# Pinning the loads in need order, folding the second DFT axis once more, a one-step inverse root, and a new stage order in a Sinkhorn attention, Fourier mixing and MLP kernel

## The chip, the cores and the metric

The kernel runs on one core of one Trainium2 chip. The metric is the device time of one execution in microseconds (us), lower is better. Each version was executed several times, and medians are quoted. A profile is of one execution, whose span can differ by some us from the median of the timed ones (before: span 369.3, median 371.6).

The engines are called as in the profile: PE is TensorE (matmuls), PEld its weight loads, DVE is VectorE, ACT is ScalarE, POOL is GpSimd and SP is SyncE. GpSimd and SyncE are the two engines that issue transfers here, each through its own queue.

## The reference, cut to what matters

Four batches, eight heads, a sequence of 768 in 8 blocks of 96, head width 64. A Sinkhorn iteration on `sort_net` gives block weights P, with which the blocks of k and v are mixed. Attention runs within each block. Its output, laid out as 768 x 512 per batch, goes through a two-dimensional Fourier transform (the real part is kept), a residual, a normalisation and an MLP.

```python
for _ in range(5):                       # Sinkhorn, (4, 8, 8, 8)
    P = exp(P - max(P)); P = P / sum(P, -1); P = P / sum(P, -2)
k_sorted = einsum('bhij,bhjcd->bhicd', P, k_b)
v_sorted = einsum('bhij,bhjcd->bhicd', P, v_b)
attn = softmax(q_b @ k_sb.T / 8)         # 96 x 96 in each block
x = (attn @ v_sb) -> (4, 768, 512)
mixed = real(fft(fft(x, axis=1), axis=2))
u = x + mixed
un = (u - mean(u)) / sqrt(var(u) + 1e-6)
out = u + relu(un @ w_ch1) @ w_ch2       # 512 -> 2048 -> 512
```

## The kernel before: the parts that matter

The program is written as a set of generators (attention, FFT with normalisation, MLP, value mix), and at build time a scheduler that simulates the engines decides the order of the instructions on each engine. Each engine then runs its list strictly in that order. An instruction may be held to the place where it was written with `tc.keep_in_program_order`. The kernel before never uses this, so the scheduler places its loads too.

The loads of the kernel before, in the order written. The 514 KB table `tab`, which the Fourier transform of the block means needs, and the first weights come late in the program text.

```python
pw  <- sort_net                                   # SyncE
def load_qk(b, hf):                               # GpSimd: half of one batch's k, then q, 384 KB each
    ...nc.gpsimd.dma_start(t..., src[b, 4*hf:4*hf+4]...)
load_qk(0, 0)
idh, idf, cm, cmh                                 # SyncE, small constants
for n in range(8):                                # SyncE, v of batches 0 and 1 (first half of the rows)
    nc.sync.dma_start(v32[hf][:, 12*qq:12*qq+12, :], vv[0:128, 12*n:12*n+12, :])
cdb, sdb, erow, vrow                              # SyncE, tables of the second DFT and others
load_qk(0, 1)
csa, sna, lt, rrow                                # SyncE; L240 loads lt, L243 one row of rb (rrow)
# ... Sinkhorn, block mean, value mix ...
tab = cload("tab", [128, 2, 2, 257], F32)         # SyncE, the last table written
# ... in the attention of batch 0:
if (b, hp) == (0, 2):
    for c in range(4): nc.gpsimd.dma_start(w1sb[:, c, :], ...)        # 512 KB each
    for c in range(4): nc.gpsimd.dma_start(w2sb[:, 4*c:4*c+4, :], ...)
# [...]
v1[hf] <- second half of v's rows                 # SyncE, for batches 2 and 3
```

The code calls the second half of v's rows "v1", the prediction "batch 1's v". It is the second pair of batches.

The second DFT, one product of 128 rows at a time (24 in the whole kernel), accumulates five 512-wide matmuls in one PSUM bank. PSUM is TensorE's output memory:

```python
ps = pf([128, DM])                                              # DM = 512
nc.tensor.matmul(ps, lt[:, 128*T:128*T+128], rb, start=True, stop=False)
for c in range(4):
    lh = ys[c][g][:, 128*tt:128*tt+128]
    rh = cdb[:, c, :] if c < 2 else sdb[:, c - 2, :]
    nc.tensor.matmul(ps, lh, rh, start=False, stop=(c == 3))     # L725
u = rt[:, T, :] * RSC + ps                                       # VectorE, L728
bn_stats, bn_aggr                                                # VectorE
```

The inverse root of the normalisation is a Newton chain on 128x3 values, three small steps on VectorE and then on GpSimd:

```python
nc.gpsimd.tensor_scalar(x, x, -0.5, None, op0=ALU.mult)
for _ in range(3):
    nc.gpsimd.tensor_tensor(z, y, y, op=ALU.mult)
    nc.gpsimd.tensor_tensor(z, z, x, op=ALU.mult)
    nc.gpsimd.tensor_scalar(z, z, 1.5, None, op0=ALU.add)
    nc.gpsimd.tensor_tensor(y, z, y, op=ALU.mult)
nc.gpsimd.tensor_tensor(z, mv[:, :, 0], y, op=ALU.mult)
nc.gpsimd.tensor_scalar(nm, z, -1.0, None, op0=ALU.mult)         # L680
```

The second half of v is prepared on VectorE (a tree of additions for the block mean, then eight subtractions of it, L873), and no MLP work is emitted before that is done.

The softmax here doesn't subtract the row's maximum and nothing guards it: scores larger than these inputs give would overflow.

## Time and profile before

| | before |
|---|---|
| median of the timed runs | 371.64 us (370.59 to 373.28, 4 runs) |
| TensorE busy | 305.4 us, 83% of the span |
| VectorE busy | 220.8 us |
| first MLP matmul starts at | 129.58 us |
| from there to the end | 240 us, TensorE busy 230 |

The head of the page has one line of busy times, with the share of the span and the number of instructions, and then rows in which each digit is the busy share of one fortieth of the span (9.2 us) in tenths. In the row PEclk the digits are the granted TensorE clock in tenths of full speed. The page of the kernel before:

```profile
PE 305.4 (83%) x2452; PEld 186.0 (50%) x2452; DVE 220.8 (60%) x507; ACT 138.5 (38%) x249; POOL 43.7 (12%) x155
...
PE   0989500864885789999998999998999999999995
...
PEclk9998955775589699999999999999999999999999
```

The row PE has a hole in slices 6 and 7, counted from 1, and is full from slice 16 on. The clock falls to 5 in and after the hole. The view of stretches (windows) of the same kernel gives busy times by engine; the number in brackets counts instructions, and the last three columns are the granted clock, the DMA share and the bandwidth:

```profile
core 0: us, PE busy (x) PEld busy (x) DVE busy (x) ACT busy (x) POOL busy (x), PEclk, DMA share, GB/s
0.00:42.00 42.00, 29.75 (x248) 20.26 (x248) 25.25 (x72) 22.50 (x40) 11.66 (x26) 0.96 1.07 238
42.00:65.00 23.00, 0.11 (x1) 0.14 (x2) 0.65 (x1) 0.67 (x1) 0.00 (x0) 0.57 0.87 226
65.00:130.00 65.00, 45.97 (x515) 33.27 (x516) 51.20 (x112) 34.79 (x62) 7.75 (x21) 0.73 0.29 44
130.00:369.30 239.30, 229.55 (x1691) 132.36 (x1689) 143.68 (x324) 80.55 (x147) 24.25 (x108) 1.00 0.11 33
```

From 42 to 65 us the engines do next to nothing while the transfers run at 226 GB/s. From 130 us on TensorE is busy for 96% of the time: there only less TensorE work helps. What TensorE waited for, longest first (engine, tile and line, what released it: total us, times, longest):

```profile
PE pf_575 L508 <- DMA tab_sb<-k_tab: 23.1, 1, 23.1
PE pm_139 L252 <- DMA v_82<-in_v_dram: 9.8, 1, 9.8
PE pf_1268 L704 <- ACT un_1250 L692: 5.5, 1, 5.5
```

The 23 us hole is one wait for one table. The chain of waits, the work that ended last followed backwards, gives start, duration and what; "SPq" is the queue of SyncE:

```profile
27.77 7.63 SPq L243
...
36.55 14.09 SPq L243
50.68 14.07 DMA tab_sb<-k_tab
...
96.08 5.21 DVE vcx L873 x6
...
121.44 0.82 ACT un_1250 L692
```

The table was issued at 50.68 us only, and needed 14.07 us to land. Ahead of it in SyncE's list stand the issues of two rows of 1 KB each (L243), and issuing them took 7.63 and 14.09 us: the engine stood in the issue itself. The list of transfers (what, issuing queue, KB each, median us from issue to landing) shows what else was under way:

```profile
w1sb<-in_moe_w_ch_dram POOLq DMA_DIRECT2D x4, 512.0 KB, 23.4
w2sb<-in_moe_w_ch_dram POOLq DMA_DIRECT2D x4, 512.0 KB, 32.3
...
k_70<-in_k_dram POOLq DMA_DIRECT2D x1, 384.0 KB, 5.6
```

The scheduler hoisted the MLP weights, written in the middle of attention 0, to 5.3 to 22.5 us of GpSimd's list, 100 us before they are used and ahead of batch 1's k and q. So 4 MB of weights share the transfer engines with everything needed in the first 50 us. Last, the timeline of GpSimd around the first inverse root (start, duration, engine, line, operation, tile):

```profile
117.33 0.19 POOL L675 TENSOR_TENSOR nz_1113<-ny_1112 128x3 f32<-128x3 f32 x1
...
121.17 0.23 POOL L680 TENSOR_SCALAR nm_1114<-nz_1113 128x3 f32<-128x3 f32 x1
```

The chain takes about 4.1 us from 117.33 us, and ScalarE's `un` at 121.44 waits for it. The timeline of TensorE in the second DFT of the last batch shows the pace of the 512-wide products. The duration of a pipelined matmul overlaps the next one, so the distance between starts is what it costs:

```profile
298.68 0.38 PE L725 MATMUL pf_3780<-vcx,yr_3539 128*128 128x512 f16 x1
298.90 0.38 PE L725 MATMUL pf_3780<-vcx,yr_3554 128*128 128x512 f16 x1
```

That is about 0.216 us each, and 1.08 us for five.

### The profile page before, as it was taken

Reading aid. Unit: us, or ns where it says so; the run is one execution under the profiler, and the core shown is the slowest. Engines: PE = TensorE matmul, PEld = TensorE weight load, DVE = VectorE, ACT = ScalarE, POOL = GpSimd, SP = SyncE. Lnnn points to the kernel's source line nnn. Section 1 sums busy time; section 2 is a strip of 40 time slices with the busy share of each in tenths; the row PEclk is TensorE's granted clock in tenths of the full one; section 3 lists DMA queues with packets and bytes.
Section 4 is the critical chain, followed back from the end, with each engine's and each line's share of the span. In section 5 each row is a group of like instructions: output and inputs, shape, how many; then the busy total and the mean of one; then the engine's idle time right before and its main releaser. Section 6 shows DMA issues by size and latency. Waiting matters only on the chain.

```text
span 369.3 us, 6087 instructions
## 1 busy us (share of the span) xinstructions
PE 305.4 (83%) x2452; PEld 186.0 (50%) x2452; DVE 220.8 (60%) x507; ACT 138.5 (38%) x249; POOL 43.7 (12%) x155
## 2 busy tenths in 40 slices
PE   0989500864885789999998999998999999999995
PEld 0448400752543667666643555664455555454552
DVE  3477500399988596447986644579473286563542
ACT  1647600371648688715302585630124212022100
POOL 7111000010004104000012300002011020021000
PEclk9998955775589699999999999999999999999999
DMA  8999987060335100514001101000100100100102
GB/s 155 320 265 225 210 219 250 27 105 0 44 45 66 22 0 6 83 57 78 9 0 58 41 2 51 36 2 0 59 28 3 58 28 2 57 30 28 57 2 85
DMA packets 18477, 25.95 MB, mean 70 GB/s; under 512 B 1737, under 2 KB 12685, under 8 KB 18449
## 3 DMA queue, kind: packets, MB, share of 16 engines
q0 software_dynamic: 11136, 10.49, 18.3%
q1 hardware_dynamic: 7314, 15.08, 11.5%
q8 instruction: 19, 0.31, 0.4%
q14 instruction: 8, 0.07, 0.1%
HBM read 29.37 MB, written 6.29 MB: 97 GB/s over the span
## 4 chain that ended last, share of the span: by engine, by line
PE 57%; DVE 19%; DMA 12%; SPq 7%; issue 2%; ACT 2%; POOL 1%; DVEq 0%; ACTq 0%
SPq L243 6%; DMA vcx<-k_sdb 4%; DMA tab_sb<-k_tab 4%; DMA v_82<-in_v_dram 2%; DVE vcx L873 2%; PE pm_3075 L773 1%; DVE r_540 L425 1%; PE pm_3013 L773 1%; PE pf_575 L508 1%; PE pm_2172 L773 1%; PE pm_2918 L773 1%; PE pm_4212 L773 1%; PE pm_2322 L773 1%; PE pm_3791 L773 1%; PE pm_4039 L773 1%
## 5 line engine op out<-in xcount | busy, mean ns | idle before, releaser
L756 PEld LDWEIGHTS <-w1sb 128*128 128x128 f16 x512 | 49.2, 98 | 36.6 <-issue 5.1
L508 PE MATMUL pf_575<-tab_sb,atp_537 128*64 128x129 f32 (+1 forms) x16 | 3.7, 405 | 23.1 <-DMA tab_sb<-k_tab 23.1
L465 PEld LDWEIGHTS <-vcx 128*128 128x128 f16 x128 | 18.1, 181 | 5.4 <-issue 2.3
L165 DVE CAST vsf<-pm_502 96x512 f16<-96x512 f32 x1 | 0.8, 799 | 27.7 <-PE pm_502 L468 27.7
L252 PE MATMUL pm_139<-v_82,idf_sb 128*128 128x512 f32 x12 | 7.7, 812 | 9.8 <-DMA v_82<-in_v_dram 9.8
L508 PEld LDWEIGHTS pf_575<-tab_sb,atp_537 128*64 128x64 f32 x16 | 3.1, 218 | 23.4 <-issue 23.4
L163 ACT CAST vsf<-pm_492 96x512 f16<-96x512 f32 x1 | 0.8, 786 | 25.2 <-PE pm_492 L468 25.2
L252 PEld LDWEIGHTS pm_139<-v_82,idf_sb 128*128 128x128 f32 x12 | 3.1, 267 | 13.6 <-issue 12.5
L468 PEld LDWEIGHTS <-vbn 128*128 128x128 f16 x64 | 8.7, 136 | 0.7 <-DVE bdv_1_291 L440 0.7
L773 PEld LDWEIGHTS <-hr_4077 128*128 128x128 f16 x48 | 4.7, 98 | 5.5
L773 PEld LDWEIGHTS <-hr_2224 128*128 128x128 f16 x48 | 4.7, 98 | 5.6
L773 PEld LDWEIGHTS <-hr_3663 128*128 128x128 f16 x48 | 4.7, 98 | 5.5
L773 PEld LDWEIGHTS <-hr_1704 128*128 128x128 f16 x48 | 4.6, 98 | 5.2
L773 PEld LDWEIGHTS <-hr_3127 128*128 128x128 f16 x48 | 4.6, 98 | 5.1
L773 PEld LDWEIGHTS <-hr_3898 128*128 128x128 f16 x48 | 4.6, 98 | 5.1
L692 ACT ACTIVATE un_3291<-u_2960,nm_3108,ny_3106 128x512 f16<-128x512 f32 x1 | 0.8, 813 | 16.8 <-POOL nm_3108 L680 16.8
L368 PEld LDWEIGHTS <-ksb_109 64*128 64x128 f16 x128 | 3.8, 97 | 6.5 <-issue 4.3
L413 PEld LDWEIGHTS <-ebuf_101 97*128 97x128 f16 x96 | 5.7, 108 | 2.6 <-DVE ebuf_101 L390 2.0
L692 ACT ACTIVATE un_2388<-u_2057,nm_2205,ny_2203 128x512 f16<-128x512 f32 x1 | 0.8, 813 | 16.5 <-POOL nm_2205 L680 16.5
L260 ACT CAST vcx<-v_82 128x768 f16<-128x768 f32 x4 | 3.3, 832 | 9.7 <-DMA v_82<-in_v_dram 9.7
L773 PEld LDWEIGHTS <-hr_3365 128*128 128x128 f16 x48 | 4.6, 98 | 4.5
L773 PEld LDWEIGHTS <-hr_2467 128*128 128x128 f16 x48 | 4.2, 98 | 4.7 <-issue 0.2
(1428 smaller groups left out, 896.4 us busy)
## 6 DMA issues: line engine op xcount, KB each, us to landing
w1sb<-in_moe_w_ch_dram POOLq DMA_DIRECT2D x4, 512.0 KB, 23.4
w2sb<-in_moe_w_ch_dram POOLq DMA_DIRECT2D x4, 512.0 KB, 32.3
v_82<-in_v_dram SPq DMA_DIRECT2D x4, 384.0 KB, 6.6
v_83<-in_v_dram SPq DMA_DIRECT2D x4, 384.0 KB, 13.2
v_524<-in_v_dram SPq DMA_DIRECT2D x2, 768.0 KB, 18.0
v_527<-in_v_dram SPq DMA_DIRECT2D x2, 768.0 KB, 18.9
tab_sb<-k_tab SPq DMA_DIRECT2D x1, 514.0 KB
k_70<-in_k_dram POOLq DMA_DIRECT2D x1, 384.0 KB, 5.6
```

What stands on the lines that cost most here:

```text
L243: nc.sync.dma_start(rb[96:97, :], cn["rrow"].ap())
L252: nc.tensor.matmul(psm.rearrange("p c d -> p (c d)"), idf, v32[n // 6][:, 8 * (n % 6):8 * (n % 6) + 8, :].rearrange("p c d -> p (c d)"), s ...
L260: nc.scalar.copy(vcp[:, 2 * n:2 * n + 2], v32[hf][:, 12 * qq:12 * qq + 12, :].rearrange("p (c r) d -> p c r d", r=6))
L368: nc.tensor.matmul(pss[h2][:, j, :], ks[rows, 4 * g + j].rearrange("p r c -> p (r c)"), qt[rows, :, cc])
L413: nc.tensor.matmul(po[:, 65 * T:65 * T + 96], e[:, S * g + 256 * tt + 128 * n: S * g + 256 * tt + 128 * n + 128], vsf[:, vi:vi + 96], star ...
L425: nc.vector.tensor_tensor(rt[:, :, D * h:D * h + D], po3[:, :, 0:D], rz[:, :, None].broadcast_to([128, 6, D]), op=ALU.mult)
L465: nc.tensor.matmul(ps[:, dd, :], vcx[:, :, d], bd, start=True, stop=(t == 1))
L468: nc.tensor.matmul(ps[:, dd, :], vbn[:, d:d + 1].broadcast_to([128, 128]), bd, start=False, stop=True)
L508: nc.tensor.matmul(psr[64 * o:64 * o + 64, cs], atp[:, par, c].rearrange("p b g -> p (b g)"), tab[:, o, c, cs], start=(c == 0), stop=(c == 1))
L756: nc.tensor.matmul(ps, w1sb[:, c, 128 * fc:128 * fc + 128], ut[:, c, :], start=(c == 0), stop=(c == 3))
L773: nc.tensor.matmul(ps, hr[:, fc, 128 * tt:128 * tt + 128], w2sb[:, fc, :], start=(fc == 0), stop=(fc == 15))
L873: nc.vector.tensor_tensor(vcp[:, 2 * n:2 * n + 2], v1[hf][:, 12 * qq:12 * qq + 12, :].rearrange("p (c r) d -> p c r d", r=6), vbs[1][:, 0: ...
```

## The change

Its stated intent has four parts: loads pinned in the order of need; the second DFT axis folded once more, with even and odd outputs computed apart; the inverse root by one GpSimd `pow`; and FFT 0 emitted ahead of attention 1. With the first part comes another treatment of the second half of v: it is loaded on GpSimd's queue behind the weights, in two halves of 1.5 MB through one buffer, cast on ScalarE, and its mean is taken out by extra matmuls instead of VectorE subtractions. The core of the diff, cut:

```diff
+    def start(ins):
+        return tc.keep_in_program_order(ins)
     load_qk(0, 0)
-    idh = cload(...) ; idf ; cm ; cmh
+    load_qk(0, 1)
+    pack ...                                  # the small constants in one transfer
-    for n in range(8):                        # v, 384 KB each
+    for n in range(4):                        # v, 768 KB each
         ...
+    start(nc.sync.dma_start(tab, cn["tab"].ap()))       # table, now ahead of the DFT's tables
+    start(nc.sync.dma_start(dtab, cn["dtab"].ap()))
     [...]
-                if (b, hp) == (0, 2): ...w1sb, w2sb...
     [...] after the Sinkhorn and the first half of the value mix:
     load_qk(1, 0)
     for n in range(16): v_mix(0, n)
+    for c in range(4): start(nc.gpsimd.dma_start(w1sb[:, c, :], ...))
+    load_qk(1, 1)
+    for c in range(4): start(nc.gpsimd.dma_start(w2sb[:, 4*c:4*c+4, :], ...))
     [...] second half of v:
+        for hf in range(2):
+            sv = wt([128, 48, D], F32, "hrB", 1, "v32")
+            start(nc.gpsimd.dma_start(sv, vv[128:256, 48*hf:48*hf+48]))
+            ... four casts on ScalarE, a tree of adds on VectorE (L865) ...
     [...] second DFT:
-            nc.tensor.matmul(ps, lt..., rb, start=True, stop=False)
             for c in range(4):
                 lh = ys[c][g][:, 128*tt:128*tt+128]
-                nc.tensor.matmul(ps, lh, rh, start=False, stop=(c == 3))
+                nc.tensor.matmul(ps[:, c % 2::2], lh, dtab[:, c, :],     # 256 wide, every second column
+                                 start=(c == 0), stop=False, ...)
+            nc.tensor.matmul(ps, lt..., rb, start=False, stop=True, ...)
     [...] inverse root:
-            (the Newton chain)
+            nc.gpsimd.tensor_scalar(mv[:, :, 1], mv[:, :, 1], 1e-6, None, op0=ALU.add)
+            nc.gpsimd.tensor_tensor(y, mv[:, :, 1], mhalf, op=ALU.pow)
+            nc.gpsimd.tensor_tensor(nm, mv[:, :, 0], y, op=ALU.mult)
+            nc.gpsimd.tensor_scalar(nm, nm, -1.0, None, op0=ALU.mult)
     [...] stage order:
+            while b == 1 and not gate1():     # m = 3: (0, 1) in uns, the second half of FFT 0 is normalised
+                yield None
```

The fold also adds VectorE steps in front of the first DFT (sums and differences of the lower and upper quarter of the axis), and moves scratch tiles into shared buffers to make room. One more thing differs: before, all MLP work is held at build time until the second half of v is ready; after, only the second group of batch 0 is.

## The prediction

> **What bounds it now.** Two regimes. From 130 us on TensorE is the limit: the table of stretches has it busy 229 of 239 us; the MLP alone costs 512 x 0.163 (four 384-wide matmuls take 0.65 us) + 384 x 0.216 = 166 us. Before 130 us it is busy only about 76 us, part of it at half clock. The list of waits gives 23.1 us in one wait for the 514 KB cosine/sine table (42 to 65 us; the clock falls to 0.50, as the Trainium skill, "TensorE: Matmul & The Clock Gate", Part 1, says of an idle array). The chain of waits then names VectorE for 72 to 117 us, with batch 1's v work (about 14 us) and attention 1 among it; then 4.4 us of GpSimd steps (117.0 to 121.4) for the inverse root. The MLP starts at 129.6 us.
>
> **What the change does.**
> - Table ahead of the weights: the 23 us hole goes. The first v load is unaffected (landed at 21 us); more v casts sit before the last Sinkhorn exponentials: +2 us.
> - Second DFT: per tile 5 x 0.216 = 1.08 us becomes 4 x 0.108 + 0.216 = 0.65 us; over 24 tiles -10 us of TensorE, all but one batch in the saturated part. VectorE folds grow by an estimated 2 us a batch.
> - Batch 1's value mix gets the mean matmuls: +2 us TensorE; VectorE loses about 6 us, ScalarE gains 6.6 us of casts.
> - Root by pow: 4.4 us becomes about 1.2 us; on the path once, for batch 0.
> - FFT 0 first: MLP starts before attention 1, whose 12 us of TensorE work moves into the MLP stretch.
>
> **Where it lands.** Without stalls the first DFT would end near 66 and the MLP start near 76 us. I expect later: GpSimd's queue is in order: batch-1 k/q loads wait for the buffer of batch 0 (about 37 us), then w1, k/q, w2, and only then half of batch 1's v. At the rate while that queue was nearly alone (190 GB/s from 42 to 50 us; 135 for k/q) this is about 37 us: v lands near 76 us. Its four casts (0.83 us each) stand on ScalarE between the second and third y of FFT 0, its tree adds on VectorE before u. So FFT 0 stalls there about 10 us. The second half of v is issued before the root of group 1 and its casts stand among the first MLP evacuations: a second stall of some 5 us. Dense MLP work starts near 99 us instead of 130.
>
> From there: remaining TensorE work is 230 (as now) + 12 (attention 1) - 9 (DFT) + 2 - 3 (first MLP pieces done in the stall) = 232; gaps and tail as now (10) plus 3 for attention 1 in between. 99 + 232 + 13 = 344.
>
> **Predicted: 345 us, 80% range 332 to 358.** Faster by over 2%: 0.96; within 2%: 0.035; slower: 0.005.
>
> **What would show it.** Right: no wait for the table over 2 us; second-DFT halves near 0.108 us apart; four GpSimd steps per root, under 1.5 us; ScalarE waiting 5 us or more for v near 70 to 80 us, and TensorE on it; first MLP matmul between 85 and 100; TensorE busy about 290 us. Wrong: v landing before 68 us (then about 330 us); stride-two PSUM writes making the halves as slow as 0.2 us (+10).
>
> **What would make it wrong.** Weights arriving at another rate; attention 1 blocking TensorE inside MLP 0; the clock staying at half in 45 to 100 us.

## The result, and the profile after

| | before | after |
|---|---|---|
| median | 371.64 us (4 runs) | 355.12 us (354.52 to 355.45, 4 runs) |
| ratio of the means | | 0.955, 95% interval 0.951 to 0.959 |
| profiled span | 369.3 | 352.4 |
| mean granted clock | 0.921 | 0.946 |
| TensorE busy | 305.4 | 305.6 |
| first MLP matmul | 129.58 | 97.27 |

A ratio here and below is the mean time of one kernel's fast runs over that of the other's fast runs of the same rounds, so it is not quite the ratio of the medians quoted. The kernel before was timed again beside every set of experiments (medians 371.72, 371.14, 372.22 and 371.55), so the sets can be compared to within some tenths of a per cent. 355.1 is the value of the changed kernel that the experiments on it are held against.

The line of busy times of the page after, then the stretches, then TensorE's waits, in the same columns as above:

```profile
PE 305.6 (87%) x2516; PEld 190.8 (54%) x2516; DVE 211.2 (60%) x464; ACT 151.4 (43%) x282; POOL 36.7 (10%) x71
```

```profile
core 0: us, PE busy (x) PEld busy (x) DVE busy (x) ACT busy (x) POOL busy (x), PEclk, DMA share, GB/s
0.00:42.00 42.00, 25.36 (x169) 17.38 (x170) 20.29 (x59) 15.70 (x29) 7.37 (x19) 0.84 0.57 157
42.00:65.00 23.00, 16.52 (x268) 14.42 (x266) 19.40 (x47) 16.38 (x31) 8.26 (x12) 1.00 1.11 194
65.00:104.00 39.00, 21.96 (x101) 13.02 (x102) 19.38 (x37) 14.17 (x24) 5.37 (x9) 0.69 0.44 120
104.00:352.40 248.40, 241.76 (x1985) 145.96 (x1982) 152.13 (x324) 105.15 (x201) 15.66 (x32) 1.00 0.17 40
```

```profile
PE pm_174 L330 <- DVE pdup_170 L321: 10.0, 1, 10.0
PE pf_875 L725 <- ACT y_855 L658: 8.2, 1, 8.2
PE pm_121 L262 <- DMA v_80<-in_v_dram: 6.6, 1, 6.6
PE pf_952 L707 <- ACT un_949 L695: 5.3, 1, 5.3
```

The hole of 42 to 65 us is gone; TensorE is busy 16.5 us there. Dense work begins near 104 us instead of 130. But dense work then lasts 248 us instead of 239, TensorE's total has not fallen, and two new waits of 10.0 and 8.2 us have come.

The first new wait goes back to a transfer. VectorE's timeline: it reaches the copy of the first q in the first of the five Sinkhorn iterations, and stands still for q with the other four behind it.

```profile
19.95 0.36 DVE L283 COPY qr_186<-q_72 128x768 f16<-128x768 f16 x1 [10.55 <-DMA q_72<-in_q_dram]
```

The transfers of the kernel after show where q is late: the first k lands 13.7 us after its issue, not 5.6, and q behind it 17.7, not 8.3.

```profile
w1sb<-in_moe_w_ch_dram POOLq DMA_DIRECT2D x4, 512.0 KB, 11.4
...
v_530<-in_v_dram POOLq DMA_DIRECT2D x1, 1536.0 KB, 17.5
...
k_70<-in_k_dram POOLq DMA_DIRECT2D x1, 384.0 KB, 13.7
```

The v rows on the other queue are now twice as long (24 x 64 values of 4 bytes a row, 6 KB, against 3 KB). The Trainium skill, "DMA: Bandwidth & Descriptors", section "Queues, rings and completion order", says that each DMA engine alternates between its queues packet by packet. If longer rows make larger packets, which no run here shows, they leave less to the other queue. The 13.7 against 5.6 us would fit that, but SyncE also issues v earlier than before (1.62 against 3.05 us), with its tables close behind (from 4.95 us). The second k and q behind k on its own queue are hardly a difference: the kernel before issued them at 3.85 and 4.58 us, the kernel after at 2.95 and 3.68. No run takes these apart, so why k is late stays open.

The second new wait is ScalarE's. In its timeline the casts of the second half of v stand between two evacuations of FFT 0:

```profile
77.54 3.03 ACT L269 CAST vcx<-v_530 128x768 f16<-128x768 f32 x4 [7.80 <-DMA v_530<-in_v_dram]
80.48 0.48 ACT L658 ACTIVATE y_855<-pf_848 128x386 f16<-128x386 f32 x1
```

The second half of the rows gets the same treatment from 99.18 us on, among the first evacuations of the MLP.

TensorE's timeline in the second DFT is the line that decides the largest term of the prediction. The products are half as wide, and start as far apart as before:

```profile
282.47 0.42 PE L725 MATMUL pf_3722<-vcx,yr_3493 128*128 128x256 f16 x1
282.69 0.42 PE L725 MATMUL pf_3722<-vcx,yr_3508 128*128 128x256 f16 x1
```

Last, GpSimd's four root steps, and VectorE's step at the same time:

```profile
100.53 0.20 POOL L682 TENSOR_TENSOR nm_994<-mv_917,ny_993 128x3 f32<-128x3 f32 x1
100.81 1.81 POOL L683 TENSOR_SCALAR nm_994<-nm_994 128x3 f32<-128x3 f32 x1
```

```profile
100.77 1.76 DVE L865 TENSOR_TENSOR v_930<-v_930 128x1536 f32<-128x1536 f32 x1 [1.62 <-ACT vcx L269]
```

The same kind of step took 0.25 us in the first root (at 91.58 us) and 1.81 us here, ending just after VectorE's add. The Trainium skill, "SBUF — State Buffer", section "Who interferes with whom", says that a VectorE instruction with two inputs in SBUF, the on-chip memory, contends with a GpSimd instruction that reads SBUF, and calls the ports that they share an exclusive lock. The trace agrees: the add started at 100.77 us, the GpSimd step at 100.81, and they ended at 102.53 and 102.62.

### The profile page after: what moved, and what is told of

It reads as the page before. It is cut to its first block, busy times and chain, and to the rows that moved or that the text cites. A ratio compares the mean times of both kernels' runs of the same rounds, so it can differ in the third digit from the quotient of the medians.

```text
span 352.4 us, 6094 instructions
## 1 busy us (share of the span) xinstructions
PE 305.6 (87%) x2516; PEld 190.8 (54%) x2516; DVE 211.2 (60%) x464; ACT 151.4 (43%) x282; POOL 36.7 (10%) x71
## 4 chain that ended last, share of the span: by engine, by line
PE 65%; issue 11%; DMA 9%; DVE 6%; POOL 4%; ACT 3%; POOLq 0%; DVEq 0%
DMA v_530<-in_v_dram 5%; DMA k_70<-in_k_dram 4%; PE pm_1169 L781 1%; PE pm_1251 L781 1%; PE pm_2324 L781 1%; PE pm_3063 L781 1%; PE pm_1377 L781 1%; PE pm_2923 L781 1%; PE pm_3197 L781 1%; PE pm_4138 L781 1%; PE pm_3569 L781 1%; PE pm_4100 L781 1%; PE pm_3965 L781 1%; PE pm_3733 L781 1%; PE pm_3527 L781 1%
## 5 line engine op out<-in xcount | busy, mean ns | idle before, releaser
L476 PEld LDWEIGHTS <-vcx 128*128 128x128 f16 x128 | 20.0, 172 | 1.1 <-issue 0.2
L425 PEld LDWEIGHTS <-eb_87 97*128 97x128 f16 x384 | 17.8, 97 | 2.8 <-issue 1.1
L262 PE MATMUL pm_121<-v_80,pack 128*128 128x512 f32 x12 | 7.2, 768 | 6.6 <-DMA v_80<-in_v_dram 6.6
L478 PEld LDWEIGHTS <-vbn_303 128*128 128x128 f16 x64 | 8.7, 136 | 0.5 <-issue 0.4
L865 DVE TENSOR_TENSOR v_530<-v_530 128x1536 f32<-128x1536 f32 (+2 forms) x3 | 3.3, 1089 | 9.1 <-ACT vcx L269 9.1
L478 PEld LDWEIGHTS <-vbn_965 128*128 128x128 f16 x64 | 8.3, 130 | 0.3
L262 PEld LDWEIGHTS pm_121<-v_80,pack 128*128 128x128 f32 x12 | 2.9, 256 | 10.0 <-issue 10.0
L781 PEld LDWEIGHTS <-hrB_4003 128*128 128x128 f16 x48 | 4.7, 98 | 5.5
L781 PEld LDWEIGHTS <-hrB_3099 128*128 128x128 f16 x48 | 4.7, 98 | 5.6
L781 PEld LDWEIGHTS <-hrB_3605 128*128 128x128 f16 x48 | 4.7, 97 | 5.6
L781 PEld LDWEIGHTS <-hrA_3321 128*128 128x128 f16 x48 | 4.8, 100 | 5.4
L781 PEld LDWEIGHTS <-hrA_3824 128*128 128x128 f16 x48 | 4.6, 97 | 5.5
L781 PEld LDWEIGHTS <-hrA_2453 128*128 128x128 f16 x48 | 4.5, 98 | 5.1
L781 PEld LDWEIGHTS <-hrB_1521 128*128 128x128 f16 x48 | 4.5, 99 | 4.9 <-issue 0.2
L781 PEld LDWEIGHTS <-hrA_999 128*128 128x128 f16 x48 | 4.4, 98 | 4.7
L283 DVE COPY qr_186<-q_72 128x768 f16<-128x768 f16 x1 | 0.4, 360 | 10.6 <-DMA q_72<-in_q_dram 10.6
L773 ACT ACTIVATE hrA_3824<-pm_3825 128x384 f16<-128x384 f32 x1 | 0.5, 492 | 14.2 <-PE pm_3825 L764 14.2
L773 ACT ACTIVATE hrB_3605<-pm_3606 128x384 f16<-128x384 f32 x1 | 0.5, 492 | 13.7 <-PE pm_3606 L764 13.7
```

Of the source, the lines that this page charges most:

```text
L262: nc.tensor.matmul(psm.rearrange("p c d -> p (c d)"), idf, v32[n // 6][:, 8 * (n % 6):8 * (n % 6) + 8, :].rearrange("p c d -> p (c d)"), s ...
L283: nc.vector.tensor_copy(qr, q16[:, 2 * hl:2 * hl + 2].rearrange("p h r d -> p r h d"))
L425: nc.tensor.matmul(po[:, 65 * T:65 * T + 96], e[:, S * g + 256 * tt + 128 * n: S * g + 256 * tt + 128 * n + 128], vsf[:, vi:vi + 96], star ...
L476: nc.tensor.matmul(ps[:, dd, :], vcx[:, :, d], bd, start=True, stop=False)
L478: nc.tensor.matmul(ps[:, dd, :], vbn[t][:, d:d + 1].broadcast_to([128, 128]), bd, start=False, stop=True)
L773: nc.scalar.activation(hr[:, fc, :], ps, AF.Relu)
```

## The experiments

Twelve kernels were run. All gave correct results. "After with ..." changes the kernel after, "before with ..." the kernel before.

My theory at the outset: the table's wait and the weights ahead of it account for the gain; the fold saves no TensorE time because it writes every second column; and the two new waits eat part of what the loads gave. Rivals: the pipeline sets another limit on the half-wide products, whatever the layout; the stage order is what brought the MLP forward; the new waits cost nothing because other work would take their place.

### 1. The fold, with contiguous halves (after with)

```diff
-                nc.tensor.matmul(ps[:, c % 2::2], lh, dtab[:, c, :],
+                nc.tensor.matmul(ps[:, 256*(c % 2):256*(c % 2) + 256], lh, dtab[:, c, :],
                                  start=(c == 0), stop=False, skip_group_check=True)
             nc.tensor.matmul(ps, lt[:, 128*T:128*T+128],
-                             rb,
+                             rb.rearrange("p (m n) -> p n m", n=2),
                              start=False, stop=True, skip_group_check=True)
-            nc.vector.scalar_tensor_tensor(u, rt[:, T, :], RSC, ps, ...)
+            nc.vector.scalar_tensor_tensor(             # the reader interleaves the halves
+                u.rearrange("p (m n) -> p m n", n=2), rt[:, T, :].rearrange("p (m n) -> p m n", n=2),
+                RSC, ps.rearrange("p (n m) -> p m n", n=2), ...)
```

Expected:

> The kernel after, but each tile's even and odd outputs of the second DFT are written to two contiguous halves of the PSUM bank, and the add that reads them puts them back in order. In the kernel after the 256-column matmuls start 0.21 us apart, like 512-column ones. Theory (the stride-two write halves the rate): they start near 0.11 us apart in the warm stretch, TensorE busy falls by 8 to 10 us, the time falls to 345 to 348 us. Rival (the weight load or the moving operand sets 0.21 us, whatever the write): spacing and time stay, 355 us within 1.

Measured: 347.55 us, ratio 0.9345 (0.9313 to 0.9376) against before, so 7.6 us under the kernel after. TensorE is busy 298.6 us instead of 305.6, which is 7.0 less and a little short of the 8 to 10 expected. The timeline of TensorE shows four products of 256 and then the one of 512:

```profile
270.73 0.60 PE L725 MATMUL pf<-vcx,y 128*128 128x256 f16 x4
271.16 0.39 PE L728 MATMUL pf<-rb,lt 97*128 97x512 f16 x1
```

The four take 0.43 us from the first start to the start of the next product, 0.108 us each, where the stride gave 0.21. So without the stride the width sets the pace here, and the stride took the whole saving. The Trainium skill, "Advanced Engine Details and Errata", section "PSUM Cachelines", says just that: lines of 8 bytes, and "Any non-contiguous AP significantly slows down matmuls". The runs agree and give the size: a factor of two at a stride of two. VectorE can read the interleaved layout in the same step that it takes anyway, so the repair cost nothing that shows in the time.

### 2. The first half of the late v ahead of the second k and q and of w2 (after with)

```diff
+    sv0 = wt([128, 48, D], F32, "hrB", 1, "v32")
+    start(nc.gpsimd.dma_start(sv0, vv[128:256, 0:48]))     # now before load_qk(1, 1) and w2
```

Expected:

> The kernel after, but the first half of batch 1's v is requested ahead of the second batch-1 k/q load and of w2. Theory (FFT 0 is held up by that load): the 8.2 us wait of TensorE for the third y goes; ScalarE may wait 2 to 4 us for v inside attention 0 instead; the first MLP matmul moves from 97 to about 91 us, the time falls to 348 to 351 us. Rival (the first MLP is bound by something else that comes as late, as w2 or the second half of v): under 2 us of gain.

Measured: 352.49 us, ratio 0.9477 (0.9457 to 0.9497), 2.6 us under the kernel after, between the theory and the rival. v landed at 64.19 us instead of 77.5. But the scheduler put the casts into attention 0, again at a place where ScalarE waits for the transfer (5.98 us, ending at 64.19), and TensorE then waited 6.1 us for an exponential of the attention. The first MLP matmul came at 96.07 us instead of 97.27, not at 91 as expected. The wait moved more than it went.

### 3. The first two q copies held behind the Sinkhorn steps (after with)

```diff
-        nc.vector.tensor_copy(qr, ...)
+        ins = nc.vector.tensor_copy(qr, ...)
+        if b == 0 and hp < 2:
+            start(ins)
```

Expected:

> The kernel after, but the first two copies of q are pinned on VectorE behind the Sinkhorn steps. Theory (VectorE stands 10.6 us in front of a q that has not landed, and Sinkhorn with it): Sinkhorn ends near 18 us instead of 27.5, the value mix starts near 26 instead of 34, every later load moves up by 6 to 8 us, and the time falls to 347 to 350 us. Rival (the start is bound by the k and q loads themselves): the wait moves to TensorE and the time stays within 2 us.

Measured: 350.37 us, ratio 0.9404 (0.9368 to 0.9439), so 4.7 us under the kernel after. The Sinkhorn steps end at 19.9 us instead of 27.7, and the first MLP matmul starts at 93.37 us instead of 97.27. So of the 7.8 us some 3 are lost again on the way; VectorE has a new wait there, 6.1 us for a q, which ends at 33.29 us. So a copy placed too early in an in-order list was worth about 5 us of the whole kernel.

### 4. Attention 1 no longer held behind FFT 0 (after with)

```diff
-        m = 3
+        m = 0
```

Expected:

> The kernel after with attention 1 again emitted as soon as it can be, as in the kernel before. Theory (putting FFT 0 first starts the MLP sooner): the first MLP matmul comes 10 us or more later than 97 us and the time rises by 4 us or more. Rival (TensorE idles about 20 us between 60 and 100 us in the kernel after, and attention 1 would fill that hole for nothing): the MLP starts later, but with attention 1 done, and the time stays within 3 us of 355 or falls.

Measured: 357.47 us, ratio 0.9614 (0.9596 to 0.9633), 2.3 us over the kernel after. The first MLP matmul came at 108.65 us, 11 us later than in the kernel after, and the total moved by 2.3. TensorE did attention 1's work in that time, though it was no busier: 25.0 us from 65 to 109 us, against 27.0 in the kernel after. This falls on the side of the rival: the stage order decides when the MLP starts, but little of the time. The start of the MLP is not a measure of the gain by itself.

### 5. The late v on SyncE's queue, behind the tables, in two buffers (after with)

```diff
+    sv1 = [wt([128, 48, D], F32, "hr" + "BA"[hf], 1, "v32") for hf in range(2)]
+    for hf in range(2):
+        start(nc.sync.dma_start(sv1[hf], vv[128:256, 48*hf:48*hf+48]))
     [...] MLP, before its first buffer is taken:
-            if (b, g) == (0, 1):
+            if b == 0:
                 while not v1ok[0]: yield None
```

The last lines hold both groups of batch 0's MLP until v is ready, since the first group's buffer now holds half of v.

Expected:

> The kernel after, but both halves of batch 1's v are requested on SyncE's queue behind the tables, into the two buffers that batch 0's v has left; the DMA engines are nearly idle from 27 to 41 us. No load is then late for its casts; the casts (6 us of ScalarE) and sums (6 us of VectorE) fall into attention 0. Theory (the late v costs the kernel after about 8 us before FFT 0's second stage and 4 us in the first MLP): no wait for v over 1 us, first MLP matmul near 89 to 92 us without a stop after it, time 346 to 350 us. Rival (what is gained is lost to the casts and sums in attention 0, as in the run with the early half): 351 us or more.

Measured: 350.24 us, ratio 0.9428 (0.9399 to 0.9457), 4.9 us under the kernel after and just outside the upper end of what I gave. No later wait for v is left, and the first MLP matmul starts at 94.25 us, not at 89 to 92. The stall of FFT 0 was real, but its 8.2 us of TensorE waiting were worth 4.9. The casts now stand in attention 0 (ScalarE, 51.28 to 57.87 us); that they take the rest is likely, but no run shows it.

### 6. Repairs 1, 3 (for all four q copies of batch 0) and 5 together (after with)

The edit is the union of the three diffs, with the condition of the third widened to `if b == 0`.

Expected:

> The kernel after with the three corrections at once: contiguous halves in PSUM (alone 7.5 us), all copies of batch 0's q pinned on VectorE behind what is traced before them (the first two alone 4.7 us), batch 1's v on SyncE's queue. If the three are separate pieces of the one chain they add: 355.1 - 7.5 - 5 - 7 = 335.6, so 333 to 339 us. If they hide behind each other: 341 us or more.

Measured: 342.25 us, ratio 0.920 (0.9160 to 0.9241). The three repairs give 7.6, 4.7 and 4.9 alone, 17.2 in sum, and 12.9 together. VectorE's timeline points to what took the rest (number 9 tests it). It is the same fault in the next batch: the first q copy of batch 1 had been hoisted into attention 0.

```profile
49.61 0.36 DVE L283 COPY qr<-q 128x768 f16<-128x768 f16 x1 [11.60 <-DMA q<-in_q_dram]
```

TensorE waited 10.3 us for an evacuation of the value mix, which VectorE ran only after that copy.

### 7. The table alone (before with)

```diff
+    tab = const.tile([128, 2, 2, 257], F32, name="tab_sb")
+    tc.keep_in_program_order(nc.sync.dma_start(tab, cn["tab"].ap()))   # ahead of the first DFT's tables
-    tab = cload("tab", [128, 2, 2, 257], F32)
```

Expected:

> The kernel before with one thing changed: the 514 KB table is requested ahead of the first DFT's tables. It shows what the 23.1 us wait alone is worth. Theory (that hole is most of the gain of the change): the wait is gone, the MLP starts at 108 to 115 us instead of 129.6, the time is 352 to 358 us. Rival (loads that come later, as batch 1's q and v at 58 to 70 us, take the time back): 362 us or more.

Measured: 367.84 us, ratio 0.9895 (0.9855 to 0.9935). The 23 us wait for the table is gone from the list, and the time fell by only 3.3 us against the median of before beside it. TensorE's waits of this run:

```profile
PE pf L415 <- DVE ebuf L392: 11.4, 1, 11.4
...
PE pf L415 <- DVE r L427: 9.7, 1, 9.7
```

VectorE in turn waited 9.7 us for batch 1's q, until 58.85 us, and 9.4 us for the second half of v, until 72.35. The first MLP matmul came at 125.97 us, not at 108 to 115. This is the rival's case: the table was only the last thing to arrive. With the weights still near the head of GpSimd's list, the next late load takes over the hole. SyncE's timeline shows that its issues still stand where they stood in the kernel before, now behind the table instead of ahead of it:

```profile
29.09 9.24 SPq L242 DMA_DIRECT2D lt<-k_lt  x1
38.37 13.92 SPq L245 DMA_DIRECT2D rb<-k_rrow  x1
```

### 8. The old root (after with)

```diff
-            add; y = pow(mv[:, :, 1], -0.5); nm = mean * y; nm = -nm
+            (the Newton chain of the kernel before)
```

Expected:

> The kernel after with the inverse root by the old chain of small GpSimd steps. Theory (the root stands twice in front of the first MLP, 4.4 us by the old chain against 1.8 us by pow): 3 to 6 us slower than the kernel after, 358 to 361 us. Rival (other waits cover it): under 1.5 us slower.

Measured: 365.25 us, ratio 0.9838 (0.9797 to 0.9879), 10.1 us over the kernel after. I had expected 3 to 6, so this is a miss. The four-step root is worth more than the difference of two chains. Two roots stand in front of the MLP's dense part, not one. In this run the first took from 92.32 to 96.46 us and the second from 104.28 to 110.46; with `pow` they ended at 91.83 and 102.62. The first starts 2.3 us later than with `pow` (92.32 against 90.00), partly because the old chain begins with three small steps on VectorE (91.87 to 92.43). The second is also longer than the first because it meets VectorE's additions of the late v. GpSimd's and VectorE's timelines of this run:

```profile
105.63 1.58 POOL L689 TENSOR_TENSOR nz<-ny 128x3 f32<-128x3 f32 x1
```

```profile
105.40 1.76 DVE L876 TENSOR_TENSOR v<-v 128x1536 f32<-128x1536 f32 x1 [1.01 <-ACT vcx L269]
```

The first MLP matmul came 4.6 us later than in the kernel after, and the end of the second root 7.8 us later. The remaining 2.3 us fit the roots of the later batches: from 112 us on TensorE waits 4.5 us for `un` in this run (four waits), against 1.9 us (one wait) from 104 us on in the kernel after.

### 9. Best version: number 6 with every q copy and the block table pinned on VectorE (after with)

```diff
-        ins = nc.vector.tensor_copy(qr, ...)
-        if b == 0:
-            start(ins)
+        start(nc.vector.tensor_copy(qr, ...))
-        nc.vector.tensor_tensor(t, tkh..., cmh..., op=ALU.mult)      # block table
+        start(nc.vector.tensor_tensor(t, tkh..., cmh..., op=ALU.mult))
```

Expected:

> The three corrections at once, with one more: the block table and the q copies of batches 1 to 3 are pinned on VectorE too. In the run of the three, VectorE stood 11.6 us in attention 0 in front of a q copy of batch 1 that the scheduler had put ahead. Theory (that wait is what kept the three from adding up): no wait of VectorE for a q over 2 us after 30 us, the first MLP matmul near 80 to 84 us instead of 90, time 331 to 336 us. Rival (attention 0 is held by other work by then): 339 us or more.

Measured: 336.72 us, ratio 0.9048 (0.9019 to 0.9077). VectorE no longer waits for q, and the first MLP matmul starts at 83.75 us. This beats both kernels: 18.4 us under the kernel after. It is a little over the range that I gave for the theory. The q copies and the block table were pinned together, so what each is worth is not shown. The largest remaining wait of TensorE is 6.9 us in two for `un`, behind the root:

```profile
PE pf L707 <- ACT un L695: 6.9, 2, 6.3
```

### 10. The fold alone, with its strided writes (before with)

The edit is the part of the diff that folds the second axis: the tables, the VectorE sums and differences, the five matmuls as in the kernel after, and the scratch tiles moved to make room.

Expected:

> The kernel before with the fold alone (halved table, even and odd outputs written with a stride of two, as the change has it, and scratch tiles moved to make room). Theory (the stride-two write takes back what the fold saves): TensorE busy within 2 us of 305, time 370 to 374 us. Rival (the fold pays by itself): 361 to 365 us.

Measured: 377.01 us, ratio 1.0145 (1.0117 to 1.0174). TensorE is busy 306.3 us, as before. As written, this part of the change costs about 5 us in the surroundings of the kernel before, more than either theory allowed. The first MLP matmul comes 1.7 us later (131.28 us), so the larger part of the cost lies after it.

### 11. The loads alone (before with)

```diff
+    tab ... tc.keep_in_program_order(nc.sync.dma_start(tab, ...))      # as in number 7
-                        nc.gpsimd.dma_start(w1sb[:, c, :], w1v[:, c, :])
+                        tc.keep_in_program_order(nc.gpsimd.dma_start(w1sb[:, c, :], w1v[:, c, :]))
-                        nc.gpsimd.dma_start(w2sb[:, 4*c:4*c+4, :], ...)
+                        tc.keep_in_program_order(nc.gpsimd.dma_start(w2sb[:, 4*c:4*c+4, :], ...))
```

Nothing else was changed: v, the fold, the root and the stage order stay as in the kernel before.

Expected:

> The kernel before with the loads alone in need order: the table first, and the MLP weights pinned where they are written, behind batch 1's first k and q. With the table alone ahead, VectorE then stood 9.7 us before batch 1's q, which queued behind 4 MB of weights. Theory (the weights in front of everything are what the 23 us hole really was): no wait for the table or that q over 2 us, the MLP starts at 108 to 116 us, time 352 to 359 us. Rival (what the change gains comes from emitting FFT 0 first): 364 us or more.

Measured: 354.03 us, ratio 0.9508 (0.9477 to 0.9538). The first MLP matmul starts at 110.01 us, and no wait for the table or for batch 1's q is left. SyncE's timeline, at the same two issues as in number 7:

```profile
24.47 2.32 SPq L242 DMA_DIRECT2D lt<-k_lt  x1
26.83 5.73 SPq L245 DMA_DIRECT2D rb<-k_rrow  x1
```

With the weights out of the way the issues stand for 8 us instead of 23, so for 15 us it was the weights on the other queue that held SyncE's list up. Weights are not the only thing that such an issue stands for. In the kernel after, which issues its first weights at 42.69 us, it still takes 12 us:

```profile
12.12 12.14 SPq L251 DMA_DIRECT2D rb_117<-k_rrow  x1
```

These nine pinned transfers bring as much as the whole change (355.12). The table moved first is worth 3.3 us, and the weights moved after it about 14 more. The weights were not moved alone, so what the table's place is worth once they are out of the way is not shown; each hides the other.

### 12. The fold alone, with contiguous halves (before with)

The edit is number 10 with the matmuls of number 1.

Expected:

> The kernel before with the second fold alone, each half of the output written contiguously, not with a stride of two. Theory (the stride took away the whole TensorE saving, and the cost of the fold in extra VectorE steps stays): starts of the 256-wide L-products about 0.108 us apart, TensorE busy 296 to 300 us, time 366 to 371 us, so 6 to 11 under the same fold with the stride (377.0). Rival (the fold is lost through VectorE or the schedule in any case): 374 us or more although TensorE is busy less.

Measured: 370.47 us, ratio 0.9966 (0.9922 to 1.001). The time lies in the range of the theory, 6.5 us under number 10, and TensorE is busy 296.7 us instead of 305.4 before. But 8.7 us less of TensorE work moved the time by 1.1 only, within the noise. In the list of waits TensorE now waits 4.6 us for VectorE to empty PSUM of the MLP's first product, eight times (2.4 us in the kernel before):

```profile
PE pm L769 <- DVE hr L774: 4.6, 8, 1.3
```

It also waits 4.9 us for the value mix's operand, as in number 10, where the kernel before waited 1.6. Both point to VectorE, which has the extra fold steps (222.1 us busy, 220.8 before) and the subtractions that the whole change took off it. That the relief of VectorE is what lets the fold pay in the kernel after is an inference from these waits. Two rivals stand untested: ScalarE is busier too (143.2 against 138.5 us), and the scratch tiles share buffers now. No run took any of these parts away alone.

## Why the prediction was right or wrong

The predicted 345 us was 10 us low, and 355.1 lies inside the range of 332 to 358. In the span of the profile the sum reads as follows. Predicted: dense work from 99 us, 232 us of TensorE work, 13 us of gaps, 344 in all. Measured: from 104, then 241.8, then 6.6 of gaps in 248.4, so 352.4.

- **The hole for the table goes: right.** No wait for it is left. The cause was only half named, though. I wrote "Table ahead of the weights: the 23 us hole goes", and the runs show that the table's place alone is worth 3.3 us (number 7); with the weights still in front, the next late load takes the hole over. Moving weights and table together gives 18 us (number 11).
- **The second DFT: wrong, and the largest term.** The step "4 x 0.108 + 0.216 = 0.65 us; over 24 tiles -10 us of TensorE" failed. The halves cost 0.21 us apart, and TensorE was busy 305.6 us, not about 290. (The prediction's own terms, 305 - 10 + 2, give 297; with contiguous halves it was 298.6.) I had named it under what would prove me wrong ("stride-two PSUM writes making the halves as slow as 0.2 us (+10)") but did not put it into the sum. Undoing only the stride brought 7.6 us (number 1). The page named in number 1 was at hand, and so this was avoidable.
- **Root by pow: the right mechanism, with the wrong size.** I wrote "4.4 us becomes about 1.2 us; on the path once". The first root took 1.83 us, `pow` itself 0.89 and the step beside VectorE's add up to 1.81. And two roots are in front of the dense part: the part is worth 10 us, not 3 (number 8).
- **v near 76 us, and the stall of FFT 0: right.** Landing was at 77.5 us, the stall was 7.8 us on ScalarE and 8.2 on TensorE, against 10 predicted. The second stall among the MLP's first evacuations shows at 99.18 us too, but smaller: 3.0 us of casts and 1.7 us of TensorE waiting, against some 5 predicted. The worth, with both stalls removed, is 4.9 us (number 5).
- **The start-up: missed.** I allowed 2 us for more casts before the last exponentials. The trace shows 10.6 us of VectorE waiting for q, and TensorE's 10.0 us behind it (number 3: worth 4.7 us).
- **FFT 0 first: right in direction.** It is worth 2.3 us (number 4).
- **VectorE's cost of the fold: too high.** I gave 2 us a batch. Alone, the fold adds 1.3 to 2.2 us of VectorE in all and 4.5 to 4.7 us of ScalarE, which I had not counted (numbers 10 and 12).
- **TensorE's clock** rose from 0.921 to 0.946. The hole's half clock is gone (1.00 from 42 to 65 us); from 65 to 104 us it is 0.69, as in the kernel before (0.68). The Trainium skill, "TensorE: Matmul & The Clock Gate", Part 1, says that an idle array falls back to half rate. The traces agree in both kernels: 0.57 over the hole of the kernel before, and 0.69 over a stretch in which TensorE was busy 22 of 39 us.

So the range held partly by luck, because errors of opposite sign met: the saving that did not come in the DFT (+10) and the start-up (+5) against more gain from the root and fewer gaps in the dense part (6.6 instead of 13). Measured separately, the parts other than the loads come to about nothing: root and stage order bring 10.1 and 2.3; the fold as written costs 5 in the kernel before; late q and late v cost 4.7 and 4.9. This adds to a loss of about 2 us, and the kernel with the loads alone is as fast as the whole change (354.03 against 355.12 us; the intervals of the ratios overlap). These are measured in different surroundings, so the sum is only a check on the order of size.

What stays open: why the fold costs 5 us in the kernel before with TensorE equally busy, beyond the waits that point to VectorE; why the first k lands late; and what the new treatment of the second half of v (mean by matmuls, the weaker hold on the MLP) is worth, which no run changed alone.

## What to carry to other kernels

When a big hole ends with one transfer, do not take that transfer as the cause. Look at what was issued ahead of everything, for what is used last, and move both; moving only the named one can hand the hole to the next late load. An in-order engine that meets a copy for a load that has not landed stops everything behind it, so after any change of load order look for copies and casts that now stand too early. And halving a matmul's width saved time here only when its output stayed contiguous in PSUM (0.108 against 0.21 us): write the halves side by side and let the reading engine interleave them.

## What the Trainium skill lacked or had wrong

- "Advanced Engine Details and Errata", section "PSUM Cachelines", says that non-contiguous access patterns slow matmuls "significantly", without a size. Here a stride of two fp32 columns doubles the cost: 0.21 us between starts of 128x256 fp16 products against 0.108 us contiguous, 7 us of TensorE busy time over 96 such products.
- "SBUF — State Buffer", section "Who interferes with whom", is right on GpSimd blocking behind a two-input VectorE instruction. It has no example of a chain of small steps: a 128x3 GpSimd step of 0.19 to 0.25 us took 1.58 and 1.81 us when it met a 128x1536 fp32 add, and one such meeting delayed a normalisation by about 1.5 us.
- No page that I found has the cost of a `pow` step on GpSimd: 0.89 us for 128x3 fp32, against 0.19 us for a multiplication, so one `pow` is worth about four of the small steps that it replaces.
